# A fused attention and mixture kernel: group 0's k maxima and squares off TensorE, and the k maximum of later groups spread behind a gate product

## The chip, the cores and the metric

One core of one Trainium2 chip runs the program, in one launch. The metric is device time in microseconds (us). Engines: TensorE (PE, its weight loads PEld), VectorE (DVE), ScalarE (ACT), GpSimd (POOL), SyncE (SP, which issues DMAs).

## What is computed

Linear attention, then two mixtures, all in float32. The part that the change touches is the attention and the norm:

```
q_s = exp(q - max over head_dim);  q_s /= sum over head_dim + 1e-9
k_s = exp(k - max over seq);       k_s /= sum over seq + 1e-9
kv  = einsum('bhsd,bhse->bhde', k_s, v)
out = einsum('bhsd,bhde->bhse', q_s, kv)
x   = out as (4608 tokens, 512)
xn  = x / sqrt(mean(x*x) + 1e-6) * rms_g
y   = (silu(xn @ w_gate) * (xn @ w_val)) @ w_out        512 -> 1536 -> 512
z   = max(y @ w1, y @ w2, y @ w3) @ w_out2              512 -> 768 -> 512
```

with 8 batches, 8 heads, 576 positions and head_dim 64.

## The kernel before

**Tiling.** The 4608 tokens form nine groups of 512: group g below 8 is the first 512 positions of batch g, the ninth holds the 64 last positions of all batches. Heads go in four pairs p of 128 features. So a pair of a group is a 128x512 tile of q, a 128x640 tile of k (five blocks of 128 positions by 128 features; 576 positions are used) and a tile of v.

**Per pair.** `k_max` finds k's maximum per feature, `k_exp` subtracts it and takes the exp, `make_kv` multiplies kᵀ by v (five 128x129 matmuls into pk, L488; the last column is the sum), divides and leaves a 128x128 kv tile; `make_x` multiplies it by q into px and squares px for the norm; `token_rstd` sums the squares per token on PE and computes 1/sqrt on DVE in ten small rows.

Two forms of the k maximum exist. From group 1 on a copy of k with features on partitions (kT) is loaded; DVE reduces it (L455), PE spreads the maximum over the partitions by a transpose of 128x128 (L477, into pb), DVE subtracts it from PSUM (L478) and ACT takes the exp (L479). Group 0 has no kT: DVE takes the maximum over the five blocks (L449), PE transposes (L452), DVE reduces (L453), and then PE itself makes k minus the maximum, as k times the identity plus the maximum times the negative identity (L465, L467), from which ACT takes the exp (L472). Its squares are summed by four PE matmuls of 128x1 per pair (L576).

**The loop.** A group has twelve iterations f: a gate product of twelve 128x512 matmuls (pg, L640 to L642; each operand is split in a high and a low part, xh and xl), tanh on ACT (L1003), a product on DVE (L1004), a value product of twelve more (pv), and h (L1025). The attention of the next group is fitted in between: group 1's while group 0's products run, and from group 2 on by a table, `turn_of`, which gives each pair of heads an iteration; `due(n)` lists the pairs that are n double iterations ahead of it. In even iterations of these groups `make_kv` follows the gate product; in odd ones `k_max` and `k_exp` stand ahead of it. Group 2's `make_x` stands ahead of the gate product of an even iteration. From group 2 on q is loaded with features on partitions (qT), and its maxima and sums come back as a statistics tile (stat) through DRAM: POOL subtracts (L390), ACT takes the exp (L391), POOL multiplies (L392).

**Weights.** The first mixture's weights come as 32-bit words, two per value; ACT scales one (L174, `first.scale`), DVE joins them (L179, L180, `first.join`), and ACT and DVE split the value into a high and a low part (L191, L196). The first weights of iteration f are loaded, joined and split in iteration f−1 of group 0; words of f = 0 and 1 at the start.

**Order.** A scheduler puts the instructions in a fixed order for each engine, by the order of the code and by `tc.issue_after`; at run time every engine takes its own list in that order and waits where an operand isn't there. SP's transfers keep the order of the code until the last group. After about 640 us the output product and the second mixture follow, which the change does not touch.

Of the kernel before, what the change touches and what calls it, by code (L numbers as in the profile page):

```python
# [11 lines left out]
AF = mybir.ActivationFunctionType  # L12
ALU = mybir.AluOpType
AX = mybir.AxisListType

P = 128
N = 512
# [9 lines left out]
BY_FEATURE = 2  # L27
# [23 lines left out]
EPS_RMS = 1e-6  # L51
# [4 lines left out]
def attention_moe_moe(ctx: ExitStack, tc: tile.TileContext, q, qt, k, kt, v, w1, w1_out, rms_g, w2, w2_out, out):  # L56
# [14 lines left out]
    nc = tc.nc  # L71
# [8 lines left out]
    def bank(tag, name):  # L80
        return ps.tile([P, N], F32, tag=tag, name=name)
# [36 lines left out]
    ident = one.tile([P, P], F32, tag="ident", name="ident")  # L118
# [3 lines left out]
    ones_f = one.tile([P, P], F32, tag="ones_f", name="ones_f")  # L122
# [7 lines left out]
    for i in range(2):  # L130
        t = one.tile([P, P], F32, tag=f"kv_raw{i}", name=f"kv_raw{i}")
# [175 lines left out]
    q_t, k_t, kT_t, v_t, kv8 = {}, {}, {}, {}, {}  # L307
    kmax, xraw, sacc, qrt, rstd = {}, {}, {}, {}, {}
# [129 lines left out]
        nc.vector.reciprocal(qr, qs)  # L438
        nc.vector.tensor_mul(q_t[g, p], q_t[g, p], qr.unsqueeze(2).to_broadcast([P, 8, 64]))

    most_bank = {}

    def k_max(g, p):
        if g == NB:
            return
        km = two.tile([P, 1], F32, tag="km", name=f"km_{g}_{p}")
        if g == 0:
            most = two.tile([P, P], F32, tag="kvh", name=f"most_{p}")
            nc.vector.tensor_reduce(most, k_t[g, p].rearrange("p c n -> p n c"), axis=AX.X, op=ALU.max)  # L449
            most_bank[p] = bank(f"acc{p}", f"pm_{p}")  # L450
            pm = most_bank[p][:, 0:P]
            nc.tensor.transpose(pm, most, ident)  # L452
            nc.vector.tensor_reduce(km, pm, axis=AX.X, op=ALU.max)  # L453
        else:
            nc.vector.tensor_reduce(km, kT_t[g, p], axis=AX.X, op=ALU.max)  # L455
        kmax[g, p] = km

    def k_exp(g, p):
        if g == NB:
            return  # L460
        if g == 0:
            pa = pair_bank(g, p, "pb", "a1")
            blocks = ((pa, 0, 4), (most_bank[p][:, P : 2 * P], 4, 5))
            for dst, a, b in blocks:
                nc.tensor.matmul(dst, ident, k_t[g, p][:, a:b, :], start=True, stop=False)  # L465
            for dst, a, b in blocks:
                nc.tensor.matmul(  # L467
                    dst, kmax[g, p].to_broadcast([P, P]), less.unsqueeze(1).to_broadcast([P, b - a, P]),
                    start=False, stop=True,
                )  # L470
            for dst, a, b in blocks:
                nc.scalar.activation(  # L472
                    k_t[g, p][:, a:b, :].rearrange("p c n -> p (c n)"), dst, AF.Exp
                )
            return
        pb = pair_bank(g, p, "pb", "a1")
        nc.tensor.transpose(pb[:, 0:P], kmax[g, p].to_broadcast([P, P]), ident)  # L477
        nc.vector.tensor_sub(k_t[g, p], k_t[g, p], pb[:, 0:P].unsqueeze(1).to_broadcast([P, 5, P]))  # L478
        nc.scalar.activation(k_t[g, p], k_t[g, p], AF.Exp)  # L479

    kvh, kvl, qh, ql, sqs = {}, {}, {}, {}, {}

    def make_kv(g, p):
        if g == NB:
            return
        pk = pair_bank(g, p, "pk", "a0")
        for c in range(5):
            nc.tensor.matmul(  # L488
                pk[:, 0 : P + 1], k_t[g, p][:, c, :], v_t[g, p][:, c, :], start=(c == 0), stop=(c == 4)
            )  # L490
        sm = two.tile([P, 1], F32, tag="ks", name=f"ks_{g}_{p}")
        nc.vector.tensor_scalar(sm, pk[:, P : P + 1], EPS_SM, None, op0=ALU.add)
        rs = two.tile([P, 1], F32, tag="kr", name=f"kr_{g}_{p}")
        nc.vector.reciprocal(rs, sm)  # L494
        raw = kv_raw[p % 2]
        for j in range(2):
            s = slice(64 * j, 64 * j + 64)
            if g < BY_FEATURE:
                nc.scalar.activation(raw[s, s], pk[s, s], AF.Copy, scale=rs[s, 0:1])
            else:  # L500
                nc.vector.tensor_scalar(raw[s, s], pk[s, s], rs[s, 0:1], None, op0=ALU.mult)
        if g not in WHOLE:
            kvh[g, p] = two.tile([P, P], F32R, tag="kvh", name=f"kvh_{g}_{p}")
            kvl[g, p] = two.tile([P, P], F32R, tag="kvl", name=f"kvl_{g}_{p}")
            split(kvh[g, p], kvl[g, p], raw)
        if g == 0:
            nc.sync.dma_start(kv_dram[p, :, g, :], raw)
        else:
            later.append((kv_dram[p, :, g, :], raw))
# [60 lines left out]

    def sum_squares(g, p):
        if p == 0:
            sacc[g] = [bank(f"acc{t}", f"pv_{g}_{t}") for t in range(4)]
        for t in range(4):
            s = slice(t * P, (t + 1) * P)
            nc.tensor.matmul(sacc[g][t][:, 0:1], sqs[p][:, s], ones_f[:, 0:1], start=(p == 0), stop=(p == 3))  # L576

    def token_rstd(g):

        var = one.tile([P, LINE], F32, tag="var0", name=f"var0_{g}")[:, 0:4]  # L580
        if g == 0:
            for t in range(4):
                nc.vector.tensor_scalar(
                    var[:, t : t + 1], sacc[0][t][:, 0:1], 1.0 / N, EPS_RMS, op0=ALU.mult, op1=ALU.add
                )
        else:
            pv = bank("a1" if g < BY_FEATURE else "acc2", f"pv_{g}")
            for t in range(4):
                s = sacc[g][:, t * P : (t + 1) * P]
                nc.tensor.matmul(pv[:, t : t + 1], s, ones_f[:, 0:1], start=True, stop=True)  # L590
            nc.vector.tensor_scalar(var, pv[:, 0:4], 1.0 / N, EPS_RMS, op0=ALU.mult, op1=ALU.add)
        z = one.tile([P, LINE // 2], F32, tag="z0", name=f"z0_{g}")[:, 0:4]
        nc.vector.tensor_scalar(z.bitcast(I32), var.bitcast(I32), -0.5, RSQRT_SEED, op0=ALU.mult, op1=ALU.add)
        a = one.tile([P, LINE // 2], F32, tag="a0", name=f"a0_{g}")[:, 0:4]
        for i in range(3):
            nc.vector.scalar_tensor_tensor(a, z, 0.25**i, z, op0=ALU.mult, op1=ALU.mult)
            nc.vector.tensor_mul(a, a, var)
            nc.vector.scalar_tensor_tensor(z, a, -3.0, z, op0=ALU.add, op1=ALU.mult)
        rstd[g] = z
        if g == 0:  # L600
            spread_rstd(g)
        if g not in COMPACT:
            later.append((rstd_dram[g].rearrange("(r t) -> r t", t=4), z))
# [47 lines left out]
    first = Weights()  # L651
# [21 lines left out]
            if 0 <= step - t < 4:  # L673
                stage(0, step - t)
    token_rstd(0)
    for stage in (first.scale, first.join, first.high, first.low):
        for h in range(2):
            stage(0, h)

# [215 lines left out]
    def iteration(g, nxt, f):  # L895
# [38 lines left out]
        def due(later):  # L934
            return [t for t in targets if turn_of(*t) == NF1 // 2 * g + pair + later]

        if not odd:
            for t in due(-2):
                if t[0] > BY_FEATURE:
                    make_x(*t)  # L940
            for t in due(-1):
                if t[0] > BY_FEATURE:
                    q_by_feature(*t)
                else:
                    make_x(*t)
            for t in due(0):
                q_softmax(*t)
            for t in due(1):
                put_stat(*t, 1, qrec[t])
                load_by_feature(*t)  # L950
            if due(2):
                for t in due(2):
                    load_first(*t)
                with tc.issue_after(lows[-1].ins):
                    for t in due(2):
                        first_stats(*t)
        else:
            for t in due(2):
                put_stat(*t, 0, qmax[t])
                if t[0] < NB:  # L960
                    load_second(*t)
            for t in due(1):
                spread[t] = spread_stats(*t)
            if due(2):
                with tc.issue_after(lows[-1].ins):
                    for t in due(2):
                        k_max(*t)
                        q_stats(*t)
            for t in due(1):
                k_exp(*t)  # L970
            for t in due(0):
                if t[0] == BY_FEATURE:
                    q_by_feature(*t)
                if t[0] == NB:
                    load_second(*t)
# [27 lines left out]
        nc.scalar.activation(t, pg, AF.Tanh, scale=0.5)  # L1003
        nc.vector.scalar_tensor_tensor(t, t, 1.0, pg, op0=ALU.add, op1=ALU.mult)  # L1004
        if not odd:
            for item in due(0):
                make_kv(*item)
        if nxt == BY_FEATURE and f == 10:
            spread_rstd(nxt)
            for p in range(4):  # L1010
                normalise(nxt, p)
# [381 lines left out]
```

## Time and profile before

| | us |
|---|---|
| median of 3 runs | 1506.61 (1505.65 to 1508.04) |
| the profiled execution, its own time | 1505.86 |
| its span | 1504.1 |
| busy in the span: PE, PEld | 1481.2, 1215.4 |
| busy in the span: DVE, ACT, POOL | 1058.3, 607.1, 455.5 |

The granted TensorE clock is full in all forty slices of the span. Each duration below comes from this one execution; the time of the execution is its span and about 1.8 us around it.

### The profile page before, as it was taken

To read this page: it belongs to the slowest core of one execution; us is meant where nothing else is said; L and a number is where in the kernel's file an instruction comes from. 1 tells how busy PE (TensorE), PEld (TensorE's weight loads), DVE (VectorE), ACT (ScalarE), POOL (GpSimd) and SP (SyncE) were. 2 spreads that over 40 slices of the span, in tenths; PEclk is the share of its full clock that TensorE was granted. 3 is DMA by queue.
4 is the path that set the end of the run, shared out by engine and by line. 5 is a ranking of instruction groups with operands and counts; after the bars stand their busy time and mean duration, and the time that the engine had idled before them with its cause. 6 is when DMAs were issued, how large, how long until landed. Compare 5 with 4: busy or idle time off the path is not lost.

```text
span 1504.1 us, 19788 instructions
## 1 busy us (share of the span) xinstructions
PE 1481.2 (98%) x6724; PEld 1215.4 (81%) x6724; DVE 1058.3 (70%) x1761; ACT 607.1 (40%) x1158; POOL 455.5 (30%) x383
## 2 busy tenths in 40 slices
PE   8899999999999999999999999999999999999998
PEld 5677878788888888888888888888888888888887
DVE  7998686867587864463798989658748748747622
ACT  6764443435343444332545545422422423413311
POOL 1002444444444444251365765111111111111100
PEclk9999999999999999999999999999999999999999
DMA  6868998878888968679535335265585585585572
GB/s 221 274 192 217 259 261 244 274 223 250 241 267 239 270 186 270 213 255 331 190 131 207 116 126 196 85 234 192 214 291 189 202 292 196 192 279 190 187 260 98
DMA packets 158757, 329.12 MB, mean 219 GB/s; under 512 B 31040, under 2 KB 55616, under 8 KB 158656
## 3 DMA queue, kind: packets, MB, share of 16 engines
q1 hardware_dynamic: 155200, 321.56, 66.4%
q10 hardware_dynamic: 3456, 6.29, 1.1%
q8 instruction: 53, 0.87, 0.2%
q14 instruction: 48, 0.39, 0.1%
HBM read 245.24 MB, written 82.55 MB: 218 GB/s over the span
## 4 chain that ended last, share of the span: by engine, by line
PE 67%; DVE 3%; DMA 2%; issue 1%; POOL 0%; ACT 0%; SPq 0%; DVEq 0%; ACTq 0%
PE p_a L647 4%; PE p_a L646 4%; PE p_a L648 4%; PE o_acc L647 4%; PE o_acc L646 4%; PE o_acc L648 4%; PE pv L642 3%; PE pv L640 3%; PE pv L641 3%; PE pg L640 3%; PE pg L641 3%; PE pg L642 3%; PE p_G L646 2%; PE p_G L647 2%; PE p_G L648 2%; PE o_a L646 2%
## 5 line engine op out<-in xcount | busy, mean ns | idle before, releaser
L1119 POOL TENSOR_TENSOR temps_wl<-temps_wl,temps_wh 128x512 f32<-128x512 f32 x36 | 48.2, 1339 | 348.5 <-ACT temps_wh L1118 273.8
L274 POOL TENSOR_TENSOR rooms_o<-st,rooms_o 128x256 fp32r<-128x256 f32 x77 | 62.6, 823 | 110.2 <-ACT rooms_o L273 99.7
L1004 DVE SCALAR_TENSOR_TENSOR t<-t,pg 128x512 f32<-128x512 f32 x64 | 43.8, 684 | 71.2 <-ACT t L1003 71.2
L1110 DVE TENSOR_TENSOR temps_wl<-temps_wl,p_a 128x512 f32<-128x512 f32 x72 | 49.2, 683 | 37.3 <-POOL temps_wl L1119 37.1
L429 POOL TENSOR_TENSOR q<-q,qm 128x512 f32<-128x512 f32 x30 | 34.3, 1145 | 135.5 <-DVE kr L494 82.2
L1114 ACT COPY temps_wh<-p_G 128x512 f32<-128x512 f32 x36 | 21.1, 586 | 106.0 <-PE p_G L648 105.8
L648 PE MATMUL p_a<-x_wh,chunk 128*128 128x512 f32 x160 | 62.3, 389 | 0.0
L647 PE MATMUL p_a<-x_wl,chunk 128*128 128x512 f32 x160 | 62.3, 389 | 0.0
L646 PE MATMUL p_a<-x_wh,chunk 128*128 128x512 f32 x160 | 62.3, 389 | 0.0
L646 PE MATMUL p_a<-x_wl,chunk 128*128 128x512 f32 x160 | 62.3, 389 | 0.0
L647 PE MATMUL p_a<-x_wh,chunk 128*128 128x512 f32 x160 | 62.3, 389 | 0.0
L648 PE MATMUL p_a<-x_wl,chunk 128*128 128x512 f32 x160 | 62.3, 389 | 0.0
L1025 DVE SCALAR_TENSOR_TENSOR h<-t,pv 128x512 f32<-128x512 f32 x66 | 45.2, 685 | 20.2 <-PE pv L642 18.4
L1116 DVE TENSOR_TENSOR temps_wl<-temps_wh,p_V 128x512 f32<-128x512 f32 x36 | 24.6, 684 | 43.9 <-PE p_V L648 43.9
L1003 ACT ACTIVATE t<-pg 128x512 f32<-128x512 f32 x64 | 37.8, 591 | 42.0 <-PE pg L642 38.3
L805 POOL TENSOR_TENSOR h_X<-h_Y,h_X 128x512 f32<-128x512 f32 x24 | 40.2, 1684 | 38.7 <-DVE o_xl L100 21.6
L809 POOL TENSOR_TENSOR h_Z<-h_Z,h_X 128x512 f32<-128x512 f32 x24 | 39.8, 1676 | 38.1 <-DVE h_X L802 34.2
L273 ACT CAST rooms_o<-st 128x256 fp32r<-128x256 f32 x77 | 31.5, 424 | 41.2 <-DMA w_dram<-rooms_o 21.6
L1004 DVE SCALAR_TENSOR_TENSOR rooms_o<-rooms_o,pg 128x512 f32<-128x512 f32 x42 | 28.7, 682 | 25.3 <-ACT rooms_o L1003 25.2
L807 POOL TENSOR_TENSOR h_Y<-h_W,h_Y 128x512 f32<-128x512 f32 x24 | 38.7, 1620 | 13.6 <-DMA h_W<-h_dram 12.9
L274 POOL TENSOR_TENSOR rooms_o<-rooms_o,rooms_o 128x256 fp32r<-128x256 f32 x36 | 28.8, 808 | 44.5 <-ACT rooms_o L273 36.8
L488 PEld LDWEIGHTS pk<-v,k 128*128 128x128 f32 x300 | 37.9, 190 | 5.0 <-ACT k L479 3.1
(1256 smaller groups left out, 4990.0 us busy)
## 6 DMA issues: line engine op xcount, KB each, us to landing
chunk<-w_dram SPq DMA_DIRECT2D x112, 768.0 KB, 4.4
w_dram<-rooms_o SPq DMA_DIRECT2D x113, 256.0 KB, 4.3
h_dram<-h SPq DMA_DIRECT2D x108, 256.0 KB, 4.2
stat<-stats SPq DMA_DIRECT2D x112, 128.0 KB, 5.1
words<-in_w SPq DMA_DIRECT2D x24, 512.0 KB, 6.9
chunk<-w_dram SPq DMA_DIRECT2D x48, 256.0 KB, 3.5
k<-in_k SPq DMA_DIRECT2D x30, 320.0 KB, 4.6
v<-in_v SPq DMA_DIRECT2D x30, 320.0 KB, 5.7
```

The costliest lines, as they stand in the source:

```text
L274: nc.gpsimd.tensor_sub(t[:, 1, :], src, t[:, 0, :].bitcast(F32))
L640: nc.tensor.matmul(pt, hi[:, j, s], xhs[kk], start=(kk == 0), stop=False)
L641: nc.tensor.matmul(pt, hi[:, j, s], xls[kk], start=False, stop=False)
L642: nc.tensor.matmul(pt, lo[:, j, s], xhs[kk], start=False, stop=(kk == 3))
L646: nc.tensor.matmul(pt, ah, bh, start=first, stop=False, skip_group_check=onto)
L647: nc.tensor.matmul(pt, ah, bl, start=False, stop=False, skip_group_check=onto)
L648: nc.tensor.matmul(pt, al, bh, start=False, stop=last, skip_group_check=onto)
L805: nc.gpsimd.tensor_sub(x, y, x)
L1004: nc.vector.scalar_tensor_tensor(t, t, 1.0, pg, op0=ALU.add, op1=ALU.mult)
L1025: lows.append(nc.vector.scalar_tensor_tensor(h, t, 0.5, pv, op0=ALU.mult, op1=ALU.mult))
L1110: nc.vector.tensor_add(y, x, pt)
L1119: nc.gpsimd.tensor_add(w, u2, s5)
```

## The change

In group 0, for the pairs 1 to 3, PE no longer makes k minus the maximum. It transposes the maximum, as in later groups; for pairs 1 and 2 DVE copies it to memory and POOL subtracts, for pair 3 DVE subtracts from PSUM. The squares of the four pairs are added up on POOL, and PE sums once. The kv tiles of group 0 are scaled on DVE. The first words are scaled and joined behind the last k maximum of group 0. From the third group on `k_exp` stands behind the gate product of its odd iteration, and group 2's `make_x` behind the gate product of its even one.

```diff
     def k_exp(g, p):
         if g == NB:
+            return
+        if g == 0 and p > 0:
+            pm = most_bank[p][:, P : 2 * P]
+            nc.tensor.transpose(pm, kmax[g, p].to_broadcast([P, P]), ident)
+            if p < 3:
+                nc.vector.tensor_copy(most_of[p], pm)
+                nc.gpsimd.tensor_sub(k_t[g, p], k_t[g, p], most_of[p].unsqueeze(1).to_broadcast([P, 5, P]))
+            else:
+                nc.vector.tensor_sub(k_t[g, p], k_t[g, p], pm.unsqueeze(1).to_broadcast([P, 5, P]))
+            nc.scalar.activation(k_t[g, p], k_t[g, p], AF.Exp)
             return
...
-            if g < BY_FEATURE:
+            if g == 1:
                 nc.scalar.activation(raw[s, s], pk[s, s], AF.Copy, scale=rs[s, 0:1])
             else:
                 nc.vector.tensor_scalar(raw[s, s], pk[s, s], rs[s, 0:1], None, op0=ALU.mult)
...
     def sum_squares(g, p):
         if p == 0:
-            sacc[g] = [bank(f"acc{t}", f"pv_{g}_{t}") for t in range(4)]
-        for t in range(4):
-            s = slice(t * P, (t + 1) * P)
-            nc.tensor.matmul(sacc[g][t][:, 0:1], sqs[p][:, s], ones_f[:, 0:1], start=(p == 0), stop=(p == 3))
+            sacc[g] = sqs[0]
+        else:
+            nc.gpsimd.tensor_add(sacc[g], sacc[g], sqs[p])
...
     token_rstd(0)
-    for stage in (first.scale, first.join, first.high, first.low):
+    with tc.issue_after(maxima[-1].ins):
+        for h in range(2):
+            first.scale(0, h)
+            first.join(0, h)
+    for stage in (first.high, first.low):
         for h in range(2):
             stage(0, h)
...
             for t in due(-1):
                 if t[0] > BY_FEATURE:
                     q_by_feature(*t)
-                else:
-                    make_x(*t)
...
-            for t in due(1):
-                k_exp(*t)
...
         nc.vector.scalar_tensor_tensor(t, t, 1.0, pg, op0=ALU.add, op1=ALU.mult)
         if not odd:
+            for item in due(-1):
+                if item[0] == BY_FEATURE:
+                    make_x(*item)
             for item in due(0):
                 make_kv(*item)
+        else:
+            for item in due(1):
+                k_exp(*item)
```

`BY_FEATURE` is 2; `maxima` collects the DVE instructions of L449, `most_of` the tiles that they write.

DVE in group 0, around the last maximum over blocks (`most`, from wh, which holds pair 3's k here), before:

```order
L453 TENSOR_REDUCE km_2_307<-pm_310 128x1
L179 TENSOR_SCALAR words_0_245<-words_0_245 128x512
L180 SCALAR_TENSOR_TENSOR y_509<-y_509,words_0_245 128x512
L179 TENSOR_SCALAR words_1_247<-words_1_247 128x512
L180 SCALAR_TENSOR_TENSOR y_509<-y_509,words_1_247 128x512
L417 TENSOR_REDUCE qm_3_320<-wh_0_3_249 128x8
L492 TENSOR_SCALAR ks_0_336<-pk_0_330 128x1
L449 TENSOR_REDUCE most_344<-wh_0_3_251 128x128
L494 RECIPROCAL kr_0_338<-ks_0_336 128x1
L196 TENSOR_TENSOR wl_(1, 0)_519<-y_509,wh_(1, 0)_516 128x512
```

and now (L450 is L449 of before, L504 and L506 are L492 and L494, L513 scales a kv tile, L470 is the new subtraction):

```order
L506 RECIPROCAL kr_1_359<-ks_1_357 128x1
L513 TENSOR_SCALAR kv_raw_217<-pk_1_351,kr_1_359 64x64
L417 TENSOR_REDUCE qm_3_314<-wh_0_3_249 128x8
L513 TENSOR_SCALAR kv_raw_217<-pk_1_351,kr_1_359 64x64
L450 TENSOR_REDUCE most_338<-wh_0_3_251 128x128
L179 TENSOR_SCALAR words_0_245<-words_0_245 128x512
L455 TENSOR_REDUCE km_3_337<-pm_340 128x1
L435 TENSOR_REDUCE qs_3_316<-wh_0_3_249 128x8
L470 TENSOR_TENSOR wh_0_3_251<-wh_0_3_251,pm_340 128x640
```

Four rows that join the first words stood ahead of the maximum; one of them now stands behind it, the others later still, and kv scalings stand ahead.

ACT at the start of the second group's iterations, where group 2's first k tile gets its exp (L479 before, L491 now), before:

```order
L1003 ACTIVATE t_11_1412<-pg_11_1399 128x512
L99 CAST x_2_1396<-xraw_3_1223 128x512
L479 ACTIVATE k_0_1229<-k_0_1229 128x640
L391 ACTIVATE qT_0_1304<-qT_0_1304 128x512
L1003 ACTIVATE t_0_1460<-pg_0_1447 128x512
L99 CAST qh_0_1521<-qT_0_1304 128x512
```

and now:

```order
L1008 ACTIVATE t_11_1383<-pg_11_1370 128x512
L99 CAST x_1_1362<-xraw_2_1059 128x512
L99 CAST x_2_1367<-xraw_3_1198 128x512
L391 ACTIVATE qT_0_1279<-qT_0_1279 128x512
L491 ACTIVATE k_0_1204<-k_0_1204 128x640
L1008 ACTIVATE t_0_1435<-pg_0_1422 128x512
L99 CAST qh_0_1492<-qT_0_1279 128x512
```

The exp of k stood ahead of the exp of qT; now it stands behind it.

DVE at the third pair of group 6, where k's subtraction is L478 before and L490 now (L248 to L261 prepare weights of the second mixture), before:

```order
L382 TENSOR_REDUCE qs_3_4490<-q_3_4277 128x8
L478 TENSOR_TENSOR k_2_4343<-k_2_4343,pb_2_4495 128x640
L383 TENSOR_SCALAR qs_3_4490<-qs_3_4490 128x8
L248 TENSOR_SCALAR st_19_4392<-st_19_4392 128x512
L385 RECIPROCAL qr_3_4493<-qs_3_4490 128x8
L249 SCALAR_TENSOR_TENSOR st_19_4392<-st_19_4392 128x512
L261 TENSOR_TENSOR st_19_4392<-st_19_4392 128x256
L1004 SCALAR_TENSOR_TENSOR rooms_o_1431<-rooms_o_1431,pg_11_4510 128x512
L262 TENSOR_TENSOR st_19_4392<-st_19_4392,st_18_4130 128x256
```

and now:

```order
L382 TENSOR_REDUCE qs_3_4465<-q_3_4252 128x8
L383 TENSOR_SCALAR qs_3_4465<-qs_3_4465 128x8
L248 TENSOR_SCALAR st_19_4367<-st_19_4367 128x512
L385 RECIPROCAL qr_3_4468<-qs_3_4465 128x8
L249 SCALAR_TENSOR_TENSOR st_19_4367<-st_19_4367 128x512
L261 TENSOR_TENSOR st_19_4367<-st_19_4367 128x256
L490 TENSOR_TENSOR k_2_4318<-k_2_4318,pb_2_4496 128x640
L1009 SCALAR_TENSOR_TENSOR rooms_o_1406<-rooms_o_1406,pg_11_4481 128x512
```

The subtraction has moved behind five rows, to just ahead of the gate row (L1004 before, L1009 now).

## Rows read from the trace of the kernel before

**Rows 1.** The page, part 1: busy time, share of the span, instructions.
```profile
PE 1481.2 (98%) x6724; PEld 1215.4 (81%) x6724; DVE 1058.3 (70%) x1761; ACT 607.1 (40%) x1158; POOL 455.5 (30%) x383
```

**Rows 2.** PE's waits: total us, times, longest us.
```profile
PE pk L488 <- ACT k L479: 2.6, 2, 1.9
PE pb L477 <- DVE km L455: 1.4, 1, 1.4
PE px L534 <- ACT qh L99: 0.8, 1, 0.8
PE px L535 <- DVE ql L100: 0.2, 1, 0.2
```

**Rows 3.** Timeline of PE, group 0: start us, us, engine, line, out<-in.
```profile
10.74 1.12 PE L465 MATMUL pb<-k,ident 128*128 128x512 f32 x2
13.01 0.27 PE L452 MATMUL pm<-ident,most 128*128 128x128 f32 x1
13.63 1.13 PE L465 MATMUL pb<-wl,ident 128*128 128x512 f32 x2
16.46 0.83 PE L488 MATMUL pk<-v,k 128*128 128x129 f32 x6
20.00 0.49 PE L465 MATMUL pm<-wh,ident 128*128 128x128 f32 x2
21.41 1.28 PE L488 MATMUL pk<-v,k 128*128 128x129 f32 x10
26.35 0.95 PE L576 MATMUL pv<-ones_f,sqs 128*128 128x1 f32 x8
33.28 1.02 PE L532 MATMUL px<-qrts,kv_raw 128*128 128x512 f32 x2
```

**Rows 4.** Timeline of DVE, group 0 and group 1's first k maximum.
```profile
17.85 1.24 DVE L449 TENSOR_REDUCE most<-wh 128x128 f32<-128x640 f32 x1
22.17 0.42 DVE L179 TENSOR_SCALAR words<-words 128x512 int32<-128x512 int32 x1
23.00 0.67 DVE L180 SCALAR_TENSOR_TENSOR y<-y,words 128x512 int32<-128x512 int32 x1
37.41 0.75 DVE L455 TENSOR_REDUCE km<-kT 128x1 f32<-128x576 f32 x1
```

**Rows 5.** Timeline of PE, group 1's first k product.
```profile
48.35 1.38 PE L488 MATMUL pk<-v,k 128*128 128x129 f32 x10 [1.93 <-ACT k L479]
```

**Rows 6.** Timeline of POOL, ACT and PE at group 2's first k product.
```profile
124.62 1.28 PE L488 MATMUL pk<-v,k 128*128 128x129 f32 x10
124.95 1.27 POOL L390 TENSOR_TENSOR qT<-qT,stat 128x512 f32<-128x512 f32 x1 [13.20 <-DMA stat<-stats]
126.25 0.63 ACT L391 ACTIVATE qT<-qT 128x512 f32<-128x512 f32 x1 [4.26 <-POOL qT L390]
```

**Rows 7.** Timeline of DVE, ACT and PE at group 6's third pair.
```profile
429.00 0.81 DVE L478 TENSOR_TENSOR k<-k,pb 128x640 f32<-128x640 f32 x1
429.90 0.74 ACT L479 ACTIVATE k<-k 128x640 f32<-128x640 f32 x1 [2.18 <-DVE qs L383]
431.04 1.28 PE L488 MATMUL pk<-v,k 128*128 128x129 f32 x10
431.05 0.43 DVE L261 TENSOR_TENSOR st<-st 128x256 f32<-128x256 f32 x1
```

**Rows 8.** Timeline of DVE and PE at group 7's third pair.
```profile
503.69 1.78 DVE L100 TENSOR_TENSOR xl<-xraw,xh 128x512 fp32r<-128x512 f32 x1
505.39 0.67 DVE L1004 SCALAR_TENSOR_TENSOR rooms_o<-rooms_o,pg 128x512 f32<-128x512 f32 x1
506.09 1.28 PE L488 MATMUL pk<-v,k 128*128 128x129 f32 x10
```

**Rows 9.** Groups by line on POOL: form and count | busy us, mean ns | idle.
```profile
L429 POOL TENSOR_TENSOR wh<-wh,qm 128x512 f32<-128x512 f32 x2 | 2.1, 1042 | 9.6 <-DVE ks L492 5.7 <-DVE qm L417 3.9
L554 POOL TENSOR_TENSOR sacc<-sacc,sq 128x512 f32<-128x512 f32 x15 | 21.6, 1440 | 4.8 <-ACT sq L552 4.8
```

More of the change, by code (lines that the diff above doesn't have):

```diff
@@ L439, in q_divide @@
         nc.vector.tensor_mul(q_t[g, p], q_t[g, p], qr.unsqueeze(2).to_broadcast([P, 8, 64]))
-    most_bank = {}
+    most_bank, most_of, maxima = {}, {}, []
     def k_max(g, p):
@@ L448, in k_max @@
             most = two.tile([P, P], F32, tag="kvh", name=f"most_{p}")
-            nc.vector.tensor_reduce(most, k_t[g, p].rearrange("p c n -> p n c"), axis=AX.X, op=ALU.max)
+            most_of[p] = most
+            last = nc.vector.tensor_reduce(most, k_t[g, p].rearrange("p c n -> p n c"), axis=AX.X, op=ALU.max)
+            maxima.append(last)
             most_bank[p] = bank(f"acc{p}", f"pm_{p}")
@@ L572, in sum_squares @@
         if p == 0:
-            sacc[g] = [bank(f"acc{t}", f"pv_{g}_{t}") for t in range(4)]
-        for t in range(4):
-            s = slice(t * P, (t + 1) * P)
-            nc.tensor.matmul(sacc[g][t][:, 0:1], sqs[p][:, s], ones_f[:, 0:1], start=(p == 0), stop=(p == 3))
+            sacc[g] = sqs[0]
+        else:
+            nc.gpsimd.tensor_add(sacc[g], sacc[g], sqs[p])
     def token_rstd(g):
         var = one.tile([P, LINE], F32, tag="var0", name=f"var0_{g}")[:, 0:4]
[L581 to L585, printed above, removed]
-        else:
[L587 to L591, printed above, removed]
+        pv = bank("a1" if g < BY_FEATURE else "acc2", f"pv_{g}")
+        for t in range(4):
+            s = sacc[g][:, t * P : (t + 1) * P]
+            nc.tensor.matmul(pv[:, t : t + 1], s, ones_f[:, 0:1], start=True, stop=True)
+        nc.vector.tensor_scalar(var, pv[:, 0:4], 1.0 / N, EPS_RMS, op0=ALU.mult, op1=ALU.add)
         z = one.tile([P, LINE // 2], F32, tag="z0", name=f"z0_{g}")[:, 0:4]
@@ L943, in iteration @@
                     q_by_feature(*t)
-                else:
-                    make_x(*t)
             for t in due(0):
```

## The prediction

> **What bounds the kernel now.** I read four views, from the coarse to the fine. The page's table of engines says that TensorE (PE) is busy 98% of the span [rows 1], so a change can only pay where it takes instructions off PE or ends a wait of PE, and only costs where PE waits longer. The view of PE's waits sorts its idle time by what ended it: a k product held by the exp of k 2.6 us, the transposed k maximum held by its reduction 1.4 us in a single wait, group 2's px held by its split q 0.8 and 0.2 us [rows 2]. These are small: the loop from the third group on has some 2.5 us to give. The timeline of PE over the first 35 us shows the other place, group 0, where max, subtraction and squares run as PE work [rows 3]; VectorE's (DVE) timeline beside it shows how closely that engine follows [rows 4].
>
> **The sum** is made against the profiled execution's own 1505.86 us. That stands 0.75 below the median of the three runs, 1506.61; I come back to it at the end. A change under 0.2%, 3.0 us, is about what can't be told from none.
>
> **Part 1, group 0.** Removed from PE: pair 1's subtraction block runs from 10.74 to 13.01, 2.27 us; pair 2's from 13.63 to 16.46, 2.83; pair 3's last block from 20.00 to 21.41, 1.41, after a first pair like the one of 1.13 at 13.63 [rows 3]: 7.6 together. Put back: three transposes of 128x128, at most 0.27 each. Of four bursts of squares (0.95 at 26.35) one stays: 2.9 off. So some 9.7 us of PE work goes, and that is the upper end of what part 1 can give; the lower end is nothing, if another engine holds the last px where it was.
>
> The other engine is DVE. It takes on two 128x128 copies, one 128x640 subtraction (0.81, as at 429.00 [rows 7]) and the scaling of four kv tiles that ScalarE (ACT) did; the joins of the first words go behind the last maximum. In the new order that maximum, at 17.85 for 1.24 now [rows 4], loses two pairs of word rows ahead of it (0.42 and 0.67 each [rows 4], 2.2 together) and gains the copies, four scalings and four one-column rows: about even, so I leave it at 17.85. Then come a word row, the small maximum, q's sum and the subtraction: 17.85 + 1.24 + 0.42 + 0.3 + 0.7 + 0.81 gives 21.3. Between that row and the last kv scaling, which px_3 needs, stand twenty-two DVE rows: eight of 128x512 at 0.67, three at 0.42, and eleven slight ones, which I estimate at 2.3 together, half a word row each; 9.0 in all. DVE rows start some 0.08 before the one ahead ends (503.69 + 1.78 against 505.39 [rows 8]), so 7.2, and 28.5; with 0.6 for the handovers between engines on the way, an estimate, the last px starts at 29.1 instead of 33.28: **4.2 of the 9.7 are kept**, the rest turns into PE waiting for DVE.
>
> Behind px_3 the squares now pass ACT (1.2 for copy and square), a GpSimd (POOL) add and one PE burst. For the add I take 1.4, the mean of its kind [rows 9]; 29.1 + 1.0 + 1.2 + 1.4 + 0.95 + 0.2 = 33.85, and group 1's first k maximum, behind it on DVE at 37.41 [rows 4], comes 3.5 earlier. PE gets to the burst 11 products after px_3, some 32.6, so a few tenths of new wait are in this. The maximum frees the buffer for the next loads on SP's queue, words behind them; the first k exp of group 1, for which PE waits 1.93 at 48.35 [rows 5], stands on ACT behind such a word. Issues and landings move with the maximum; of the 3.5 I keep **2.8** beyond that point, since the rows that split group 0's x do not shorten. On SP a store of kv moves ahead of group 1's kT load; its tile is scaled earlier now, so it holds nothing. The later join of the first words ends about 26.5, by the same row count, just ahead of the first product on PE: cover 0.5 us, and gone if DVE is later.
>
> The two POOL subtractions of 128x640 have no row. Their nearest is the 128x512 one of the same kind, 1.04 [rows 9]: 1.3 by size, taken, since nothing there runs unlike it; upper bound is twice that.
>
> **Part 2, the moved k maximum and group 2's px.** Removed waits: 1.4 for the transpose at group 4, and 0.8 and 0.2 for group 2's px, now behind a product [rows 2]: −2.5 with small ones. PE's work is the same. But the transpose now stands 24 products ahead of its k product where it stood 36, and, above all, the subtraction on DVE and the exp on ACT stand further back in queues that run in order. What is queued ahead of them decides. When the subtraction moves behind DVE rows that follow it today, these come forward by its length and it ends where the last of them ends today; the exp (0.74 at 429.90) adds its own.
>
> - Group 2, k_0. ACT does the exp behind the exp of qT, at 126.25 for 0.63, which waits for POOL, at 124.95, which waits for a statistics DMA [rows 6]. The exp then ends at 127.6; PE is there at 124.62. Three products that now stand ahead take 0.7 of the 3.0: **+2.3**.
> - Group 6, k_2. Behind five DVE rows, the last ending at 431.05 + 0.43 = 431.48; exp done at 432.25, PE there at 431.04 [rows 7]: **+1.2**.
> - Group 7, k_2. Behind the x splits and a gate row that ends at 506.06; exp done at 506.85, PE there at 506.09 [rows 8]: 0.8, a wait for xl that vanishes included. Group 3's has the same rows around it, group 4's fewer. Together between 0, if rows ahead get through earlier than today, and 2.0; half, **+1.0**.
>
> All other pairs keep spare time by the same count. Part 2: −2.5 + 2.3 + 1.2 + 1.0 = **+2.0**.
>
> **Sum:** −2.8 + 2.0 = −0.8, 1505.1 in the profiled execution's frame and 1505.8 in the median's. I put 1505.4 between them, with 1502.5 to 1508.5 for this case.
>
> **Rivals.**
> 1. *The new waits do not come.* The queues run ahead of PE by more than I count, and the moved exps end in time; all that is removed stays. For it: of the 28 k exps most end two to six us ahead of PE today. Against: 431.04, where 0.4 is spare now [rows 7]. Then −2.8 − 2.5: 1500.6; up to 1.5 lower if DVE clears the twenty-two rows sooner.
> 2. *Slower: the statistics DMA does not move with the prologue.* Place: group 2's k_0. POOL waits 13.20 us idle for that landing [rows 6], so the exp of qT, and from now on the k exp behind it, run when the DMA lands, not when PE is early. If the transfers of groups 0 and 1 fill the DMA engines, it lands at its old time, and the 2.8 of part 1 are lost there: 2.3 − 2.5 + 1.2 + 2.0 = +3.0, 1509.6; slower from the point where it lands at or after its old time and the k_2 waits come in full. Against: its issue follows stores that follow PE.
> 3. *POOL is held by DVE.* The same POOL add of 128x512 takes 1440 ns on average, where the broadcast subtraction of that size takes 1.04, and DVE's split takes 1.78 at 503.69 where a row of that size takes 0.67 [rows 8, 9]. Beside POOL, then, either can stretch, and in group 0 both are now on the way to px_3: subtractions at up to 2.7, an add up to 0.9 longer, 2.3 of part 1 lost, 1507.7. [...]
> 4. *The prologue is bound elsewhere and nothing moves there*: part 1 nothing, part 2 as counted: +2.0, 1508.2.
>
> **How the numbers follow.** Forecast 0.40; rival 1 0.30, since the counts on both queues rest on one execution; rival 2 0.15; rivals 3 and 4 0.15 together. Faster by over 0.2% is below 1503.6: nearly all of rival 1 and a little of the forecast, 0.32. Slower is above 1509.6: most of rival 2 and a little of the others, 0.14. Within it, 0.54. The range reaches to 1499.5, rival 1 with part of its extra, and to 1509.5, rival 2's price; beyond lie a tenth on either side.
>
> **What would show it.** Right: the last px of group 0 near 29 us with PE idle ahead of it until DVE rows end; group 1's first k product some 3 us earlier; new waits of a k product on the exp of k at group 2 (some 2.9 us), group 6 (1.2) and three under 1; the wait of 1.4 gone. Wrong: a sum of those waits as small as the 2.6 of now (rival 1), POOL's wait for statistics ending at 124 to 125 as before (rival 2), POOL rows of 2 us before 33 us (rival 3), px_3 still at 32 or later (rival 4).

## The result, and the profile after

The changed kernel took **1517.70 us** (median of 6 runs, 1509.78 to 1518.97), against 1505.87 for the kernel before beside it: a ratio of **1.0073, with a 95% interval of 1.0057 to 1.0089**, 9 to 13 us slower. The profiled execution took 1517.21, its span is 1515.4. The forecast was 1505.4, in a range of 1499.5 to 1509.5.

PE's busy time stayed where it was [rows 1], although PE now has 45 matmuls fewer, since part of its work ran slower (group 2's first k product took 2.52 us where it took 1.28, at a granted clock of 0.50, below). Its idle time in the span grew from 22.9 to 34.2 us. The page, part 1, of the changed kernel:

```profile
PE 1481.2 (98%) x6679; PEld 1215.6 (80%) x6679; DVE 1067.6 (70%) x1769; ACT 605.7 (40%) x1147; POOL 464.6 (31%) x388
```

The view of PE's waits of the changed kernel (total us, times, longest):

```profile
PE pk L500 <- ACT k L491: 8.7, 6, 3.0
...
PE pv L595 <- POOL sacc L566: 2.7, 1, 2.7
PE px L544 <- ACT sqs L556: 1.5, 1, 1.5
```

The exp of k now holds PE for 8.7 us in six waits where it held it for 2.6 [rows 2]. A wait for POOL's add ahead of group 2's sum of squares (2.7 in one) is new. The waits of [rows 2] for the transposed maximum of the loop and for group 2's px are gone.

How far the changed kernel is behind, read as the start of each gate product's first row in the two timelines of PE (worked out from those rows; "iteration 1.2" is the third iteration of the second group):

| gate product | before | after, later by | what lies between |
|---|---|---|---|
| 1.0 | 120.87 | +0.62 | group 0's part |
| 1.2 | 134.77 | +4.91 | group 2's k_0 |
| 1.8 | 175.07 | +3.24 | px_1's wait gone |
| 1.10 | 188.18 | +9.59 | group 3's k_0, group 2's sum of squares |
| 3.1 | 285.54 | +7.91 | the wait of 1.4 gone |
| 4.10 | 415.40 | +7.27 | |
| 5.1 | 434.95 | +11.39 | group 6's k_1 and k_2 |
| 8.11 | 707.64 | +11.03 | |

Three places lose 4.29, 6.35 and 4.12 us; what was gained between them takes 4 off. In the first two the waits make up little more than half of what was lost (in the first once x's wait of before, 0.70 below, is taken off). The view by stretches of the changed kernel (its length, the busy time and instructions of PE, PEld, DVE, ACT and POOL, then granted clock, DMA share, GB/s):

```profile
20.00:30.00 10.00, 8.12 (x32) 5.80 (x33) 9.46 (x23) 7.51 (x14) 1.55 (x1) 0.66 0.42 134
126.00:136.00 10.00, 7.90 (x28) 6.78 (x29) 4.46 (x10) 3.29 (x6) 3.03 (x3) 0.66 0.77 263
136.00:184.00 48.00, 47.20 (x230) 39.11 (x229) 33.53 (x69) 21.85 (x43) 21.27 (x21) 1.00 0.88 232
184.00:198.00 14.00, 11.28 (x48) 8.84 (x47) 12.16 (x30) 5.83 (x11) 6.58 (x6) 0.88 0.89 220
420.00:450.00 30.00, 26.34 (x126) 21.39 (x125) 26.04 (x52) 13.37 (x28) 11.25 (x11) 1.00 0.89 254
```

Before, the clock is 1.00 in all five stretches, as in this one:

```profile
126.00:136.00 10.00, 10.00 (x46) 8.17 (x45) 6.92 (x16) 4.46 (x8) 2.52 (x3) 1.00 0.86 293
```

Now it falls to 0.66, 0.66 and 0.88 in the first, second and fourth. The page's line of forty slices can't show this, since it gives tenths and reads 9 throughout for both kernels; the mean over the span is 1.000 before and 0.993 now. PE's timeline at group 2's k_0 shows what such a stretch is:

```profile
124.21 0.39 PE L645 MATMUL pv<-x,wh_(1, 0)_491 128*128 128x512 f32 x1
124.44 0.39 PE L646 MATMUL pv<-x,wh_(1, 0)_491 128*128 128x512 f32 x1
124.66 0.39 PE L647 MATMUL pv<-x,wl_(1, 0)_494 128*128 128x512 f32 x1
128.10 2.52 PE L500 MATMUL pk<-v,k 128*128 128x129 f32 x10 [3.05 <-ACT k L491]
130.27 0.78 PE L645 MATMUL pv<-x,wh_(1, 0)_491 128*128 128x512 f32 x1
130.84 0.63 PE L646 MATMUL pv<-x,wh_(1, 0)_491 128*128 128x512 f32 x1
131.27 0.63 PE L647 MATMUL pv<-x,wl_(1, 0)_494 128*128 128x512 f32 x1
...
133.83 0.41 PE L647 MATMUL pv<-x,wl_(1, 0)_494 128*128 128x512 f32 x1
134.08 0.40 PE L645 MATMUL pg<-x,wh_(1, 1)_556 128*128 128x512 f32 x1
```

PE waits 3.05 us for the exp of k; then the ten matmuls of pk take 2.52 us, where they took 1.28 [rows 6], and the products behind them follow each other every 0.43 us, where at 124.21 to 124.66 it is 0.23. The granted clock is 0.50 from 128 to 133 us, and the spacing is back at 0.25 only at 133.8. In PE's timeline of before, a wait for x stands a little ahead of this place:

```profile
121.96 0.50 PE L641 MATMUL pg<-x,wh_(1, 0)_516 128*128 128x512 f32 x1 [0.70 <-DVE x L100]
```

Of the 4.29 us between iterations 1.0 and 1.2, 3.05 are the new wait, 0.70 come off for x's wait, which is gone, 0.69 for three px products that moved behind the mark; 2.6 are left for the clock. By iteration 1.3, where the px products stand ahead of the mark again, the same place has cost 4.9.

### The profile page after: what moved, and what is told of

It is laid out like the page before. It is cut to its first block, busy times and chain, and to the rows that moved or that the text cites. A ratio compares the mean times of both kernels' runs of the same rounds, so it can differ in the third digit from the quotient of the medians.

```text
span 1515.4 us, 19699 instructions
## 1 busy us (share of the span) xinstructions
PE 1481.2 (98%) x6679; PEld 1215.6 (80%) x6679; DVE 1067.6 (70%) x1769; ACT 605.7 (40%) x1147; POOL 464.6 (31%) x388
## 4 chain that ended last, share of the span: by engine, by line
PE 76%; DVE 5%; DMA 2%; issue 1%; SPq 1%; ACT 0%; POOL 0%; DVEq 0%; POOLq 0%
PE pv L645 5%; PE pv L647 5%; PE pv L646 5%; PE pg L645 5%; PE pg L646 5%; PE pg L647 4%; PE p_a L652 4%; PE p_a L651 4%; PE p_a L653 4%; PE o_acc L653 3%; PE o_acc L652 3%; PE o_acc L651 3%; PE p_G L651 2%; PE p_G L652 2%; PE p_G L653 2%; PE o_a L651 2%
## 5 line engine op out<-in xcount | busy, mean ns | idle before, releaser
L1009 DVE SCALAR_TENSOR_TENSOR t<-t,pg 128x512 f32<-128x512 f32 x64 | 43.8, 684 | 77.8 <-ACT t L1008 77.7
L500 PE MATMUL pk<-v,k 128*128 128x129 f32 x300 | 40.9, 282 | 9.4 <-ACT k L491 8.7
L1008 ACT ACTIVATE rooms_o<-pg 128x512 f32<-128x512 f32 x42 | 24.9, 592 | 56.5 <-PE pg L647 56.4
```

Of the source, the lines that this page charges most:

```text
L500: nc.tensor.matmul(pk[:, 0 : P + 1], k_t[g, p][:, c, :], v_t[g, p][:, c, :], start=(c == 0), stop=(c == 4))
```

## The experiments

Each ratio is to the kernel before on the same chip, with its 95% interval. The kernel before itself took 1502.73 to 1515.91 us in these sets of runs, so that differences under 2 us are separated neither within a set nor between two.

**The two halves, and the two moves of the loop.** Edits: the change with the hunks of the loop undone; those hunks alone on the kernel before; of them `k_exp`'s lines alone; and `make_x`'s alone:

```diff
-            for t in due(1):
-                k_exp(*t)
...
+        else:
+            for item in due(1):
+                k_exp(*item)
```

> Group 0's part alone; k_exp and group 2's px stand where they stood before. Theory A (the loop's moves made the waits, and a wait of some 3 us is followed by a stretch of half clock): the gate products of group 0 start 0.3 to 0.6 us later than before, as in the changed kernel, and nothing is added behind: 0 to +1.5 us against before; low granted clock near 20 to 28 us only. Theory B (group 0's later words and statistics make the loop's waits): most of the 11 us are here, +6 us or more. Theory C (group 0's part is a gain that a clock stretch at 20 to 28 us eats): also near 0, but px_3 comes earlier than 33.3 us on an execution without the low clock.

> Both moves in the loop (k_exp and group 2's px behind the gate product) on the group 0 of before. Theory A: +9 to +11 us, with PE waiting some 3 us for the exp of k at group 2's k_0, 2.7 us for POOL's add at group 2's sum of squares, and a low clock behind each. Theory B: under +3 us.

> k_exp moved alone. Theory A: the waits on the exp of k stay (group 2's k_0 3 us, single ones of about 1 us in groups 3, 4, 6, 7), the wait for POOL's add at the sum of squares of group 2 goes, and the wait of 1.0 us for group 2's px of before comes back: +6 to +8 us. If the low clock behind 185 us belongs to the sum of squares, it is gone here.

> Group 2's px moved alone. Theory A: px's wait of 1.0 us goes (-1.6 us at the start of that iteration), the sum of squares of group 2 waits 2.7 us for POOL's add near 185 us, with some low clock behind it: +1 to +3 us. If the wait for POOL is made by the later k exps of that group instead, the move is a gain of 1 to 2 us.

| | ratio | us against 1509.4 |
|---|---|---|
| group 0's part alone | 0.9984 (0.9970 to 0.9998) | −2.4 |
| the loop's moves alone | 1.0046 (1.0030 to 1.0062) | +6.9 |
| k_exp moved alone | 1.0066 (1.0043 to 1.0090) | +10.0 |
| group 2's px moved alone | 1.0023 (1.0009 to 1.0037) | +3.5 |

Group 0's part is a small gain, the loop's moves make the loss: theory B falls. The loop alone came out under the +9 to +11 expected, and k_exp alone over its +6 to +8; both moves cost by themselves, and do not add (13.5 as a sum, 6.9 together). The px move shows its wait in the waits view of that run: the sum of squares 3.6 us, at 185 us, with group 2's px free of its own.

```profile
PE pv L590 <- POOL sacc L554: 3.6, 1, 3.6
```

Why POOL's add is late there is in ACT's and POOL's timelines of the changed kernel:

```profile
184.84 0.68 ACT L558 ACTIVATE xraw<-px,gain 128x512 f32<-128x512 f32 x1
186.95 0.63 ACT L430 ACTIVATE q<-q 128x512 f32<-128x512 f32 x1 [1.43 <-POOL q L429]
187.49 0.58 ACT L564 ACTIVATE sq<-px 128x512 f32<-128x512 f32 x1
```

```profile
185.87 1.04 POOL L429 TENSOR_TENSOR q<-q,qm 128x512 f32<-128x512 f32 x1 [0.55 <-DVE qm L417]
188.21 1.27 POOL L566 TENSOR_TENSOR sacc<-sacc,sq 128x512 f32<-128x512 f32 x1 [1.29 <-ACT sq L564]
```

The last px is done near 181.9 us. Its square (L564) stands on ACT behind the exp of a q tile (L430), which waits 1.43 us for POOL; POOL's add (L566) follows, and the sum on PE starts at 189.54. In PE's timeline of before 26 rows stood between px_3 and the sum, now 13.

**One row of ACT, in both directions.** In the changed kernel the exp of k was put ahead of the exp of qT for group 2's first pair; later the reverse was done to the kernel before, where nothing else moved but the k product by three products and one DVE row:

```diff
+            with tc.issue_after(exps[t].ins):
+                q_softmax(*t)
```

> The changed kernel as it is, on the chip of the three beside it, as their measure. +5 to +11 us against before by every theory.

> The changed kernel with one pair of ACT rows exchanged: group 2's first exp of k ahead of the exp of qT. Theory A (the exp of k waits for a row that waits for the statistics): PE's wait of 3.05 us at 128 us falls under 1.5 us, no low clock from 126 to 134 us, 3 to 5 us faster than the changed kernel. Rival (the k exp itself is late, by DVE's subtraction at 123.2 us): the wait stays over 2 us and the time within 1 us.

> The kernel before, with one pair of ACT rows exchanged and nothing else moved but the k product's place by three products: group 2's first exp of k behind the exp of qT, as the changed kernel has it. Theory A: PE waits 2.5 to 3.5 us for that exp near 127 us, the granted clock falls to half for some 5 us behind it, and the second gate product of that group of iterations starts 4 to 5 us later than before; of that 2 to 5 us remain at the end. Rival (the wait alone costs; the low clock is the chip's own): the wait of 3 us less the 0.7 that three products and x's wait give back, so 2.3 us later, the clock full.

The changed kernel on this chip: 1.0058 (1.0037 to 1.0079), +8.8 us. With the one exchange: 1.0045 (1.0029 to 1.0060). PE's timelines of these two executions, without and with the exchange:

```profile
126.63 2.52 PE L500 MATMUL pk<-v,k 128*128 128x129 f32 x10 [3.21 <-ACT k L491]
```

```profile
123.73 1.38 PE L500 MATMUL pk<-v,k 128*128 128x129 f32 x10 [0.57 <-ACT k L491]
```

The wait fell from 3.21 to 0.57 us, the clock stayed at 1.00 in the stretch from 126 to 136 us (0.68 without the exchange), and iteration 1.2 started 2.2 us earlier than in the kernel before, not 3.5 later: 5.7 us, of which 0.3 were there at iteration 1.0 already. Some 300 us on, group 6's k_2 waited 3.92 us in that execution, with a clock of 0.50 over the 5 us behind, and lost 2.4 us more than without the exchange; with all that came between, 4.9 us were left between the two executions at iteration 8.11. So the mechanism is shown at its place, but the 3 to 5 us expected at the end are shown by this one pair of executions only: the two medians are 0.5 us apart, and the intervals overlap.

The reverse in the kernel before gave 1.0003 (0.9994 to 1.0011): nothing.

```profile
128.06 1.38 PE L492 MATMUL pk<-v,k 128*128 128x129 f32 x10 [1.62 <-ACT k L394]
```

The wait came, by the same row, but with 1.62 us: PE was 1.1 us later at iteration 1.0 than in the kernel before, it still had x's wait ahead, and the exp ran when the statistics had landed, which in this execution took less time than in the others (6.55 us from the issue to POOL's start; below, at rival 2). No low clock followed (1.00 from 126 to 136 us); iteration 1.1 was 1.8 us later, and by 1.4 px's wait [rows 2] had taken in nearly all of it. The expected 2.5 to 3.5 us and the low clock did not occur, so this run bounds the cost of a short wait (none at the end, by the interval at most 1.7 us) and leaves that of a long one to the executions that had it.

**Fillers.** To keep PE working through the two long waits, twelve products of constants were added to the changed kernel, six ahead of each:

```diff
+        for i in range(6):
+            nc.tensor.matmul(
+                dst[:, 2 * P : 4 * P], ident, less.unsqueeze(1).to_broadcast([P, 2, P]), start=True, stop=True
+            )
```

> The changed kernel, with six 128x256 products of constants (some 2.6 us of PE work that nobody reads) ahead of group 2's first k product and six ahead of its sum of squares, where PE waited 3.05 and 2.72 us. Theory A (a wait near 3 us is followed by half clock, which costs 2 to 4 us more each time): the waits shrink to the fillers' place, the granted clock stays full from 120 to 200 us, and the time falls 3 to 5 us below the changed kernel though nothing useful was added. Rival (the waits alone cost, the clock is noise of the chip): no change, or up to 1 us slower.

1.0058 (1.0042 to 1.0073), as without. The clock was 1.00 from 126 to 136 us, as theory A has it, but the fillers also changed the order on DVE, ACT and POOL, and from 165 to 180 us new waits and a clock of 0.50 to 0.97 took what was saved. The run is inconclusive.

**Keeping what pays.** Group 0's part, and `k_exp` behind the gate product for the fourth pair of groups 3 to 7 alone:

```diff
+                if item[0] > BY_FEATURE and item[1] == 3:
+                    k_exp(*item)
```

> Group 0's part, and k_exp behind the gate product for the fourth pair of groups 3 to 7 alone, where the exp kept some 4 us of spare time in every trace with the move. Theory A: the wait of 1.4 to 1.7 us of a transposed k maximum near 285 us goes and no wait takes its place: 1 to 2 us under group 0's part alone, so 0.997 of before. Rival (the moved exps always end late): no better than group 0's part alone, 0.9984.

**0.9978 (0.9966 to 0.9991), 3.3 us under the kernel before**, and 12 us under the changed kernel beside it (medians 1507.52 and 1519.09). That is near the 0.997 expected, but it is not separated from the 0.9984 of group 0's part alone, so whether the fourth pairs' move pays or only costs nothing stays open. No transposed maximum of the loop waits for its reduction any more; the largest waits that the view still has for the later groups' form of the exp and for group 2's px are these, the first of them in group 1:

```profile
PE pk L500 <- ACT k L491: 2.7, 1, 2.7
...
PE px L546 <- ACT qh L99: 1.5, 1, 1.5
```

On this base three more things were tried, on another chip.

> Group 0's part with the fourth pairs' k_exp moved (0.9978 of before), and on ACT the exp of pair 3's k behind the two reads of px_0, ahead of which it stood waiting for DVE. Theory A: PE's wait of 1.5 to 2.2 us for px_0's square near 24 us goes, with the low clock behind it; the last px of group 0 starts 1 to 2 us earlier, and 0.5 to 1.5 us of that is kept at the first gate product. Rival (DVE's row of twenty-two rows bounds the last px anyway): under 0.5 us.

> The same base, with group 2's px behind the gate product for pairs 0 to 2 and the fourth left ahead of it, so that the sum of squares has its old distance. Theory A: the wait of 1.5 us for px_1's q near 148 us goes and the wait for POOL's add at the sum of squares stays away: 1 to 2 us under the base. Rival (POOL's add is late by its own queue, whatever the place of the last px): the wait of some 2.7 us at 183 to 190 us is there, 2 us or more above the base.

> The same base, with the subtractions of group 0's pairs 1 and 2 on DVE from PSUM (as pair 3's) in place of the copy and POOL. If DVE's rows were held by POOL's subtractions, DVE loses the rows of 1.65 us at 15.8 us: the last px at the same time or up to 1 us earlier, and the time within 1 us of the base. If DVE is bound by its row count, the two longer rows (0.81 for 0.28) put the last px 1 us later and cost up to 1 us.

> The order of ACT in group 0 and the three px moved, together. Theory A: both gains add, 2 to 3 us under the base, near 0.996 of before.

| on that base | ratio |
|---|---|
| ACT's order in group 0 | 0.9992 (0.9978 to 1.0007) |
| px of three pairs | 0.9992 (0.9982 to 1.0003) |
| subtractions on DVE | 0.9982 (0.9969 to 0.9994) |
| the first two | 0.9980 (0.9967 to 0.9993) |

None is separated from the base's 0.9978. ACT's order left 1.61 us of the wait for px_0's square and did not bring the last px forward (31.30 against 31.02 us): DVE's rows bound it, as that rival said. With three px moved, the wait for POOL stayed away, but px waited 2.91 us for its q at 175 us (3.69 at 178 with both) in place of 1.55 at 148. With the subtractions on DVE the last px came at 31.99, a microsecond later, and the time did not show it.

## Why the prediction was wrong

**The step that failed is part 2's +2.0**; the loop's moves alone measured +6.9 (4.5 to 9.4). Two terms were put at nothing, the lower clock behind a wait (0.50 over 5 us at group 2's k_0) and the add that px_3 feeds, and one wait was mis-sized. In order:

- *k_0 of group 2, "+2.3".* The wait was right, 3.05 for 3.0, and so was its chain: POOL's subtraction waited for the statistics until 125.50, ACT's exp of qT ran at 126.79, the exp of k behind it at 127.33. The price was not: the place cost 4.3, since PE's clock fell to 0.50 over the 5 us behind the wait. I had read the clock as full in the whole trace of before, which it was (a mean of 1.000), and priced every wait at its own length. Nor is the wait a fixed 3.0: with this order on ACT it came out at 1.62 to 5.03, with the landing of the statistics (below, at rival 2).
- *"All other pairs keep spare time by the same count".* They did not. The sum of squares of group 2, with px_3 moved closer to it, waited 2.72 us; I had counted px's gain and not the add that comes behind. Group 3's k_0 waited 0.80, group 6's k_1 0.99. Between iterations 1.8 and 1.10, 6.35 us went: 3.5 of waits, 0.7 of displaced px, some 2 of clock (0.88 in that stretch).
- *k_2 of group 6, "+1.2".* It waited 2.67. I had taken the DVE rows ahead of the subtraction at their times of before. But kvl, ahead of them all, waits for ACT, whose queue waits for POOL and the statistics again (0.36 us before). DVE's timeline of the changed kernel:

```profile
436.40 1.31 DVE L100 TENSOR_TENSOR kvl<-kv_raw,kvh 128x128 fp32r<-128x128 f32 x1 [1.72 <-ACT kvh L99]
437.74 0.69 DVE L1036 SCALAR_TENSOR_TENSOR h<-t,pv 128x512 f32<-128x512 f32 x1
438.35 0.68 DVE L382 TENSOR_REDUCE qs<-q 128x8 f32<-128x512 f32 x1
...
440.39 0.43 DVE L261 TENSOR_TENSOR st<-st 128x256 f32<-128x256 f32 x1
440.74 0.81 DVE L490 TENSOR_TENSOR k<-k,pb 128x640 f32<-128x640 f32 x1
```

  kvl waited 1.72 us for ACT and ran 1.31 while POOL's L392 ran from 436.26 to 437.57; before, it took 0.59 from 427.18, beside the last 0.43 us of that POOL row (426.32 to 427.61). Seven rows, the five of the prediction among them, and the subtraction stand behind it.
- *The gains, "−2.5".* About right: −1.46 at iteration 3.1, and −1.67 from 1.2 to 1.8.
- *The three small k_2, "+1.0".* Group 3's waited 0.92; group 7's and group 4's under 0.5 in this execution.

**Part 1, "−2.8", lies within what was measured** (−2.4, 0.3 to 4.5, alone), but by luck: its working was wrong. The last px started at 31.0 us in that run and 31.92 in the changed kernel, not at 29.1. Group 1's first k maximum, which was to come 3.5 earlier than 37.41, started at 36.30 and 37.45, and the maximum of group 0's last pair, left at 17.85, at 18.66 and 19.11. DVE's timeline of the changed kernel, and POOL's:

```profile
15.82 1.65 DVE L439 TENSOR_TENSOR wh<-wh,qr 128x512 f32<-128x512 f32 x1
...
28.16 1.63 DVE L581 TENSOR_TENSOR raws<-xraw,raws 128x512 fp32r<-128x512 f32 x1
```

```profile
15.38 1.54 POOL L468 TENSOR_TENSOR wl<-wl,most 128x640 f32<-128x640 f32 x1 [0.50 <-DVE most L467]
...
27.70 1.55 POOL L587 TENSOR_TENSOR sqs<-sqs 128x512 f32<-128x512 f32 x1 [7.81 <-ACT sqs L556]
```

DVE's multiplication at 15.82 ran 1.65 us where it took 0.69, while POOL's subtraction ran to 16.92; at 28.16 another ran 1.63, where its row took 0.67 to 0.68 before (L569), beside POOL's add, which ran to 29.25. This is rival 3, on DVE's side: both rows ended 0.54 to 0.55 us after POOL's. In the trace of before the split of 1.78 at 503.69 ended 0.55 after a POOL row as well, L392, which ran 1.65 from 503.27. Why a row runs longer there is not shown. Rival 3's own sign, POOL rows of 2 us, did not come: POOL's subtraction took 1.54, not 1.3, and its adds 1.28 to 1.55. In the run with the subtractions on DVE, POOL's subtraction is not there, nor is the long row. DVE's timeline there:

```profile
16.01 0.69 DVE L439 TENSOR_TENSOR wh<-wh,qr 128x512 f32<-128x512 f32 x1
...
17.92 1.24 DVE L450 TENSOR_REDUCE most<-wh 128x128 f32<-128x640 f32 x1
```

The multiplication took 0.69 again and the maximum of the last pair started at 17.92, where the prediction had it, in place of 18.69 on the base. These 0.96 us are not the whole delay: the last px came no earlier (31.99, after a px of 1.91 us in place of 1.02 at 28.06) and the run was no faster. And PE, thinned out, waited 0.66 to 1.55 us four times between 14 and 25 us; from 20 to 30 us its clock was 0.66, px at 24.33 took 2.07 in place of 1.02, and in this execution group 0's gain was gone (+0.62 at iteration 1.0; −0.86 in the execution of that part alone, with a clock of 0.83 there; −1.02 in the second profile of the changed kernel, with 1.00).

**Rival 2** named the right place and sign. Its condition did not decide: the statistics landed 6.6 to 6.7 us after their issue whether that was at 118.35 or, in the second profile of the changed kernel, at 116.72, so that in these two they do move with group 0; the wait was 3.05 and 3.21. The loss is no prologue gain that was lost, but the place itself and the clock behind it. What the prediction took as fixed is the time of this transfer. In the run of the loop's moves alone, SP's timeline and POOL's:

```profile
118.65 2.55 SPq L144 DMA_DIRECT2D stat<-stats  x4
```

```profile
127.78 1.26 POOL L390 TENSOR_TENSOR qT<-qT,stat 128x512 f32<-128x512 f32 x1 [15.14 <-DMA stat<-stats]
```

POOL started 9.13 us after the issue there, and PE waited 5.03. In the other executions with this order on ACT and without fillers it was 7.72 and a wait of 3.62 (k_exp alone), 7.30 and 3.21, 7.15 and 3.05, and 6.55 and 1.62 (the exchange in the kernel before). Why the transfer takes longer in one execution than in another stays open.

The rivals' times do not share a frame: 1500.6 counts from 1505.86, 1509.6 from 1506.61 and 1508.2 from between. Nothing turns on these 0.75 us.

**What stays open.** How much of the 11 us is clock is worked out from traces, not isolated by a run. In the profiled execution the clock of 0.66 over 10 us and 0.88 over 14 us in the loop is worth at most 3.4 + 1.7 = 5.1 us, about half of the 10.4 us lost from iteration 1.0 to 8.11. No run confirms this share: the fillers moved other rows, and the single exchange in the kernel before made no long wait. What speaks for it: of each six timed runs of the changed kernel the fastest had the highest mean clock, 1509.78 us at 0.999 against 1516.04 to 1518.97 at 0.992 to 0.994, and in the second set 1515.10 at 0.998 against 1517.13 to 1524.85 at 0.992 to 0.995. By these two the change costs some 4 to 5 us where the clock nearly holds.

## What to carry to other kernels

A move that shortens the distance between a producer and PE's use of it is priced by the in-order queues between them (here the exp of k stood on ACT behind the exp of qT, ahead of which ACT was idle for 6.24 us): walk every queue to the row that itself waits, above all for a DMA, and do so for what the moved work feeds, not only for what it waits for. Where PE is otherwise always busy, a wait of some microseconds can cost more than its length, since the work behind it can run slower (4.9 us for one of 3.05 here, with a clock of 0.50 over the next 5 us); a shorter one can cost nothing where a later wait takes it in (1.62 here). A wait that ends with a transfer has no fixed length either (1.62 to 5.03 us here). Move the parts that have slack in every trace (here one pair of four, which cost nothing), and leave the rest.

## What the runs showed of the hardware that was not expected

The clock behind a wait. In the loop, from group 1's first k product on, the eight waits of PE of 2.91 to 5.03 us in the changed kernel and the experiments were all followed by a mean clock of 0.50 to 0.69 over the next 5 us. Of the eight waits of 2.62 to 2.72 us six were (0.50 to 0.73), and two kept 1.00. Of the 34 waits of 1.35 to 2.41 us, those of the kernel before included, 13 were (0.50 to 0.71; ten of them at that first k product, near 48 us), and 21 kept 1.00, the 1.93 of the kernel before at 48.35 and the 1.62 of the exchange in it among them. The length alone does not settle it, then, and the same kernel varies by some 9 us from run to run (1509.78 to 1518.97 us).

The time of one transfer. The same statistics transfer let POOL start 6.55 to 9.13 us after its issue, and PE's wait behind it went from 1.62 to 5.03 us.
